# Fused attention and two MLPs on one core: k and q rows laid out consecutively per partition, transposes head by head, group sums of v by additions

## The chip, the cores and the metric

One core of a Trainium2 chip runs one launch. The metric is the device time of one execution in microseconds (us). All arrays are float32, except the weights and alpha, which are float64 and are read as pairs of 32-bit integers.

## What is computed

```python
q_d, k_d, v_d = q, k, v averaged over groups of 4 rows          # (4, 8, 144, 64)
out_up    = repeat(softmax(q_d k_d^T / 8) v_d, 4, rows)          # coarse attention
out_local = softmax(where(|i - j| < 4, q k^T / 8, -1e6)) v       # banded attention
x  = (out_up + out_local), heads side by side                    # (2304, 512)
x  = (silu(x w_gate) * (x w_val)) w_out                          # d_ff 1536
h  = x w_in                                                      # d_ff 2048
out = (max(h, 0) + alpha * min(h, 0)) w_out2                     # (2304, 512)
```

with q, k and v of shape (4, 8, 576, 64): four sequences, eight heads, 576 rows, 64 columns.

## The kernel before

**Units.** The attention is cut into 32 units. A unit n is one head pair (hp = n mod 4) of one block of 288 tokens; two blocks make a sequence. Units 0 to 3 are the first half of sequence 0, units 4 to 7 its second half. Units 0 to 7 run in a prologue, the others are woven into the first MLP's loop. A unit goes through these steps: `a_load` (k for the whole sequence if it is a first half, and q), `a_load_v` (v in groups of four rows), `a_load_w` (v in overlapping windows, L249, out of a DRAM copy `vwin`), `a_T` (k and q transposed, so that the 64 columns of two heads lie on 128 partitions; group sums kd and qd), `a_vd` (group sums of v), `a_QK` (L360 banded scores, L364 coarse scores), `a_EXP` (L394, L403), `a_NRM` (L427), `a_PT` (L441 transposes, L444 copies the coarse probabilities to SBUF on ACT), `a_PV` (L461 coarse, L465 banded product, then the sum L470 on DVE and the splitting into the high part xh, L474 on ACT, and the low part xl).

**Window copies.** `stage(b)` copies v of a sequence from DRAM to DRAM into overlapping windows (L260 and L266), 8 KB for each window. Those of sequence 0 come in the prologue, that of sequence 1 behind the load of block 7's w_out, those of sequences 2 and 3 behind the load of block 11's.

**Weights.** The first MLP has 12 weight blocks j, each with three tiles of 512 KB: g_j, v_j (L106) and o_j (L104). `w_split` prepares one: two activations on ACT (L129, L137), one operation on DVE, a cast on ACT (L142) and a subtraction on GpSimd, which leave the weight as the sum of two float32 replacements that TensorE takes at its fast rate. `m_g` multiplies by g_j (three matmuls of `mm3`, L488 to L490, for each of four pieces of 128 columns), takes tanh (L527) and a product u (L528, DVE); `m_v` and `m_y` follow with v_j and o_j. For the first 288 tokens, the blocks are used in order as they are prepared; for later tokens all are there.

**Slots.** The tiles of the prologue's attention lie in the SBUF slots of weight blocks 4 to 11, so those weights are loaded when the unit that held the slot is done with it (`pslot`). o11's slot belongs to no unit.

**The order of instructions.** The kernel is written in the order of the steps, but a list scheduler of the framework sets the order of each engine's queue, from its own estimate of durations; a few `issue_after` calls bind pieces of it (`gate`, `prep1`, `load8`). Each engine and each DMA-issuing queue then works through its list in order. All loads here are issued by SP (SyncE). A change of one step can therefore move instructions of all others.

**What the change touches.** The k loads (L213) and q loads (L218): one DMA for each head, in which partition p gets rows p, 96 + p, ... of the sequence, 64 numbers (256 bytes) in a piece. The transposes L306, L309 and L315 (one for both heads of 96 rows), and the copies out of PSUM behind them: L310 to L312 on ACT, L319 on DVE. The group sums of v, L344: two reductions on DVE for each of units 0 to 3.

Of the kernel before, what the change touches and what calls it, by code (L numbers as in the profile page):

```python
# [23 lines left out]
def attn_moe_moe2_kernel(  # L24
# [169 lines left out]
    def a_load(n):  # L194
        b, half, hp, blk = coords(n)
        h0, t0 = 2 * hp, half * HB
        d = hu[n] = {}
        if n >= NPRO:

            loads = [("qn", q, HB, t0)]  # L200
            if half == 0:
                loads.insert(0, ("kn", k, S, 0))
            for tag, src, rn, r0 in loads:
                t = d[tag] = ap_.tile([128, rn], F32, tag=tag, name=tag, bufs=1)
                for i in range(4):
                    nc.sync.dma_start(
                        out=t[32 * i:32 * (i + 1)].rearrange("r (m c) -> r m c", c=32),
                        in_=src[b, h0 + i // 2, r0:r0 + rn, 32 * (i % 2):32 * (i % 2 + 1)].rearrange("(m r) c -> r m c", r=32))
            return
        if half == 0:  # L210
            kn = d["kn"] = at_(n, [QB, 6, 2, D], "kn")
            for h in range(2):
                nc.sync.dma_start(out=kn[:, :, h], in_=k[b, h0 + h].rearrange("(r p) c -> p r c", p=QB))  # L213
        t = at_(n, [128, 2 * NW * 2 * D], "qv").rearrange("p (a w h c) -> p a w h c", a=2, w=NW, h=2)
        d["vw"] = t[:, 1]
        qn = d["qn"] = t[:QB, 0]
        for h in range(2):
            nc.sync.dma_start(out=qn[:, :, h], in_=q[b, h0 + h, t0:t0 + HB, :].rearrange("(r p) c -> p r c", p=QB))  # L218

    def a_load_v(n):  # L220
        b, half, hp, blk = coords(n)
# [30 lines left out]
    def stage(b, halves=(0, 1)):  # L252
# [32 lines left out]
        else:  # L285
            win(g0, g1)

    def a_T(n, A):
        b, half, hp, blk = coords(n)
        d = hu[n]  # L290
        idn = ident[:QB, :QB]
        small(n)
        qT, qd = d["qT"], d["qd"]
        nc.gpsimd.memset(qT[:, HB:HB + 8], 0.0)  # L294
        if half == 0:
            kT = kTs[hp] = ap_.tile([128, KW], F32, tag=f"kT{hp}", name="kT", bufs=1)
# [6 lines left out]
            nc.vector.transpose(out=qT[:, 0:HB], in_=d["qn"])  # L303
        elif half == 0:
            for r in range(6):
                nc.tensor.transpose(A[:, r // 3, (r % 3) * QB:(r % 3 + 1) * QB], d["kn"][:, r].rearrange("p h c -> p (h c)"), idn)  # L306
            for r in range(NW):
                dst = A[:, 1, HB + QB * r:HB + QB * (r + 1)] if r < 2 else A[:, 0, 320:320 + QB]
                nc.tensor.transpose(dst, d["qn"][:, r].rearrange("p h c -> p (h c)"), idn)  # L309
            nc.scalar.copy(out=qT[:, 0:2 * QB], in_=A[:, 1, HB:HB + 2 * QB])  # L310
            nc.scalar.copy(out=qT[:, 2 * QB:HB], in_=A[:, 0, 320:320 + QB])
            nc.scalar.copy(out=kT[:, 3:S + 3].rearrange("c (f t) -> c f t", f=2), in_=A[:, :, 0:HB])  # L312
        else:
            for r in range(NW):
                nc.tensor.transpose(A[:, 0, QB * r:QB * (r + 1)], d["qn"][:, r].rearrange("p h c -> p (h c)"), idn)  # L315
            if K["qtA"]:
                nc.scalar.copy(out=qT[:, 0:HB], in_=A[:, 0, 0:HB])
            else:
                nc.vector.tensor_copy(qT[:, 0:HB], A[:, 0, 0:HB])  # L319
        if half == 0:  # L320
            if 0 < n < NP:
                kq = kT[:, 3:S + 3].rearrange("c (g r) -> c g r", r=4)
# [13 lines left out]
    def a_vd(n):  # L336
# [2 lines left out]
            return  # L339
        if half == 0:  # L340
            vs = vss[hp] = ap_.tile([72, 2, 2, D], F32, tag=f"vs{hp}", name="vs", bufs=1)
            for f in range(2):
                if n < NP:
                    nc.vector.reduce_sum(vs[:, f], hu[n]["vd"][f].rearrange("p h (r c) -> p h c r", r=4), axis=AX.X)  # L344
                    continue
                vv = hu[n]["vd"][f].rearrange("p h (r c) -> p h r c", r=4)
                nc.gpsimd.tensor_tensor(out=vv[:, :, 0:2], in0=vv[:, :, 0:2], in1=vv[:, :, 2:4], op=ALU.add)
                nc.gpsimd.tensor_tensor(out=vs[:, f], in0=vv[:, :, 0], in1=vv[:, :, 1], op=ALU.add)
# [523 lines left out]
```

## Time and profile before

| | us |
|---|---|
| median of 3 runs | 1009.46 |
| lowest, highest | 1009.44, 1010.22 |
| the profiled execution's span | 1008.6 |
| PE (TensorE matmul) busy in it | 970.5 (96%) |
| DVE busy | 479.7 (48%) |
| ACT busy | 307.6 (30%) |
| POOL busy | 380.0 (38%) |

The profile gives the profiled execution's span and no other time of that execution. Of the span, some 160 us are the prologue and the first pass through the weight blocks, in which the attention of sequence 0, the loads and the preparation of the weights run side by side; behind it PE is nearly always busy. TensorE's granted clock is listed for each stretch as a share of its full rate.

### The profile page before, as it was taken

How to read it: one execution, taken by the hardware profiler on the slowest of the kernel's cores; microseconds unless marked ns; L12 is line 12 of the kernel's file. 1: busy time of each engine (PE TensorE's matmuls, PEld its weight loads, DVE VectorE, ACT ScalarE, POOL GpSimd, SP SyncE). 2: the span in 40 equal slices, each digit the busy share in tenths (PEclk: the TensorE clock that was granted, in tenths of full speed). 3: DMA queues.
4: the chain of work that ended last, by engine and by line, in shares of the span. 5: the costliest groups of instructions: out<-in, count | busy, mean ns of one | idle time of the engine just before them, and what ended most of it. 6: DMA issues, size and time to landing. Idle time of an engine off the chain costs nothing.

```text
span 1008.6 us, 19231 instructions
## 1 busy us (share of the span) xinstructions
PE 970.5 (96%) x7760; PEld 866.4 (86%) x7760; DVE 479.7 (48%) x1010; ACT 307.6 (30%) x699; POOL 380.0 (38%) x488
## 2 busy tenths in 40 slices
PE   5689899999999999999999999999999999999998
PEld 4488799999999999999999997888888888888897
DVE  5886874464535464545432769623222222322232
ACT  4598632222222222222223656312111111211111
POOL 6487852244322334222223436624223222322222
PEclk9799999999999999999999999999999999999999
DMA  7899731132111221111104883102000100100010
GB/s 185 254 337 340 174 89 35 27 82 56 41 38 33 70 45 41 44 23 21 41 9 141 287 255 106 32 1 79 6 0 21 53 1 1 47 7 0 1 43 21
DMA packets 135888, 77.80 MB, mean 77 GB/s; under 512 B 97401, under 2 KB 127097, under 8 KB 135033
## 3 DMA queue, kind: packets, MB, share of 16 engines
q1 hardware_dynamic: 135735, 76.57, 26.9%
q8 instruction: 60, 0.98, 0.4%
q14 instruction: 29, 0.24, 0.1%
q10 hardware_dynamic: 64, 0.01, 0.0%
HBM read 67.12 MB, written 15.73 MB: 82 GB/s over the span
## 4 chain that ended last, share of the span: by engine, by line
PE 81%; DMA 7%; DVE 4%; SPq 3%; POOL 2%; ACT 2%; issue 1%; POOLq 0%; DVEq 0%; ACTq 0%
PE y L625 7%; PE y L627 7%; PE y L626 7%; PE g L488 6%; PE v L489 6%; PE v L488 6%; PE g L489 6%; PE g L490 6%; PE v L490 5%; PE y L488 4%; PE y L490 4%; PE y L489 4%; PE h L488 3%; PE h L490 3%; PE h L489 3%; DMA raw<-in_moe_w_out_dram 3%
## 5 line engine op out<-in xcount | busy, mean ns | idle before, releaser
L613 POOL TENSOR_TENSOR gl<-t,gh 128x512 fp32r<-128x512 f32 (+1 forms) x80 | 97.1, 1214 | 250.6 <-ACT gh L612 244.3
L612 ACT CAST gh<-t 128x512 fp32r<-128x512 f32 (+1 forms) x80 | 46.1, 578 | 278.5 <-DVE t L609 238.8
L488 PE MATMUL g<-xh,w 128*128 128x288 f32 x384 | 117.7, 306 | 10.4 <-DVE u L528 5.4
L490 PE MATMUL g<-xh,w 128*128 128x288 f32 x384 | 115.0, 300 | 0.8 <-POOL qT L294 0.8
L488 PE MATMUL v<-xh,w 128*128 128x288 f32 x384 | 115.7, 301 | 0.1
L489 PE MATMUL v<-xl,w 128*128 128x288 f32 x384 | 115.1, 300 | 0.0
L489 PE MATMUL g<-xl,w 128*128 128x288 f32 x384 | 114.8, 299 | 0.0
L489 PE MATMUL y<-pl,w 128*128 128x288 f32 x384 | 113.9, 299 | 0.8 <-POOL pl L538 0.8
L625 PE MATMUL y<-w,gh 128*128 128x512 f32 x288 | 113.2, 393 | 1.0 <-ACT sy L557 1.0
L490 PE MATMUL v<-xh,w 128*128 128x288 f32 x384 | 113.3, 295 | 0.0
L490 PE MATMUL y<-ph,w 128*128 128x288 f32 x384 | 113.0, 297 | 0.0
L626 PE MATMUL y<-w,gh 128*128 128x512 f32 x288 | 112.8, 392 | 0.0
L627 PE MATMUL y<-w,gl 128*128 128x512 f32 x288 | 112.0, 392 | 0.0
L528 DVE SCALAR_TENSOR_TENSOR u<-u,g 128x288 f32<-128x288 f32 x96 | 43.3, 451 | 143.0 <-ACT u L527 142.9
L488 PE MATMUL y<-ph,w 128*128 128x288 f32 x384 | 110.9, 302 | 0.0
L538 POOL TENSOR_TENSOR pl<-u,ph 128x288 fp32r<-128x288 f32 x96 | 81.6, 850 | 56.9 <-ACT ph L537 56.5
L143 POOL TENSOR_TENSOR w<-st,w 128x512 fp32r<-128x512 f32 x52 | 70.7, 1366 | 55.6 <-ACT w L142 55.3
L488 PEld LDWEIGHTS g<-xh,w 128*128 128x128 f32 x384 | 73.3, 191 | 14.2 <-DVE u L528 7.4
L607 DVE TENSOR_SCALAR t<-h,alpha 128x512 f32<-128x512 f32 (+1 forms) x40 | 27.9, 696 | 110.7 <-PE h L490 109.5
L488 PEld LDWEIGHTS y<-ph,w 128*128 128x128 f32 x384 | 70.8, 189 | 4.5 <-issue 4.4
L490 PEld LDWEIGHTS g<-xh,w 128*128 128x128 f32 x384 | 73.6, 192 | 1.1 <-POOL qT L294 1.1
L527 ACT ACTIVATE u<-g 128x288 f32<-128x288 f32 x96 | 39.3, 409 | 115.4 <-PE g L490 109.3
(197 smaller groups left out, 2148.2 us busy)
## 6 DMA issues: line engine op xcount, KB each, us to landing
raw<-in_moe_w_out_dram SPq DMA_DIRECT2D x28, 512.0 KB
raw<-in_moe_w_in_dram SPq DMA_DIRECT2D x16, 512.0 KB
raw<-in_moe_w_gate_dram SPq DMA_DIRECT2D x12, 512.0 KB
raw<-in_moe_w_val_dram SPq DMA_DIRECT2D x12, 512.0 KB
vw<-vwin SPq DMA_DIRECT2D x48, 96.0 KB
out_dram<-os SPq DMA_DIRECT2D x18, 256.0 KB
sy<-y SPq DMA_DIRECT2D x16, 256.0 KB
y<-ys SPq DMA_DIRECT2D x14, 288.0 KB
```

The lines of the kernel that those rows point to most:

```text
L143: eng.tensor_sub(w[:, 1], st, f32(w[:, 0]))
L488: nc.tensor.matmul(o, lhi, rhi, start=first, stop=False)
L489: nc.tensor.matmul(o, lhi, rlo, start=False, stop=False)
L490: nc.tensor.matmul(o, llo, rhi, start=False, stop=last)
L527: nc.scalar.activation(out=u, in_=GV[0][:, :HB], func=AF.Tanh, scale=0.5)
L528: nc.vector.scalar_tensor_tensor(out=u, in0=u, scalar=1.0, in1=GV[0][:, :HB], op0=ALU.add, op1=ALU.mult)
L538: nc.gpsimd.tensor_sub(pl, u, f32(ph))
L612: nc.scalar.copy(out=gh[:, :n], in_=t[:, :n])
L613: nc.gpsimd.tensor_sub(gl[:, :n], t[:, :n], f32(gh[:, :n]))
L625: nc.tensor.matmul(o, gh[:, ms], ohi, start=(j == 0), stop=False)
L626: nc.tensor.matmul(o, gh[:, ms], olo, start=False, stop=False)
L627: nc.tensor.matmul(o, gl[:, ms], ohi, start=False, stop=(j == F2 - 1))
```

## The change

It alters three things. For units 0 to 7, k and q are loaded so that partition p holds consecutive rows (6p to 6p + 5 of k, 3p to 3p + 2 of q), one DMA for both heads of a unit, in pieces of 1536 and 768 bytes. Since the two heads of a row no longer lie side by side in a tile, each transpose of both heads becomes two ordinary matmuls against the identity, one for each head (`two_T`), and the copies out of PSUM write to strided places, which restores the order of the rows. For units 0 to 3, the two reductions of v become two additions of halves for the whole unit, in place and then into `vs`.

```diff
--- before.py
+++ after.py
@@ -208,14 +208,14 @@
                         in_=src[b, h0 + i // 2, r0:r0 + rn, 32 * (i % 2):32 * (i % 2 + 1)].rearrange("(m r) c -> r m c", r=32))
             return
         if half == 0:
-            kn = d["kn"] = at_(n, [QB, 6, 2, D], "kn")
-            for h in range(2):
-                nc.sync.dma_start(out=kn[:, :, h], in_=k[b, h0 + h].rearrange("(r p) c -> p r c", p=QB))
+            kn = d["kn"] = at_(n, [QB, 2, 6, D], "kn")
+            nc.sync.dma_start(out=kn.rearrange("p h r c -> p h (r c)"),
+                              in_=k[b, h0:h0 + 2].rearrange("h (p r) c -> p h (r c)", p=QB))
         t = at_(n, [128, 2 * NW * 2 * D], "qv").rearrange("p (a w h c) -> p a w h c", a=2, w=NW, h=2)
         d["vw"] = t[:, 1]
-        qn = d["qn"] = t[:QB, 0]
-        for h in range(2):
-            nc.sync.dma_start(out=qn[:, :, h], in_=q[b, h0 + h, t0:t0 + HB, :].rearrange("(r p) c -> p r c", p=QB))
+        qn = d["qn"] = t[:QB, 0].rearrange("p w h c -> p (w h c)").rearrange("p (h r c) -> p h r c", h=2, r=NW)
+        nc.sync.dma_start(out=qn.rearrange("p h r c -> p h (r c)"),
+                          in_=q[b, h0:h0 + 2, t0:t0 + HB, :].rearrange("h (p r) c -> p h (r c)", p=QB))
 
     def a_load_v(n):
         b, half, hp, blk = coords(n)
@@ -285,12 +285,17 @@
         else:
             win(g0, g1)
 
+    def two_T(dst, src, idn):
+        for h in range(2):
+            nc.tensor.matmul(dst[64 * h:64 * h + 64], src[:, h], idn, start=True, stop=True)
+
     def a_T(n, A):
         b, half, hp, blk = coords(n)
         d = hu[n]
         idn = ident[:QB, :QB]
         small(n)
         qT, qd = d["qT"], d["qd"]
+        qR = qT[:, 0:HB].rearrange("c (p r) -> c r p", r=NW)
         nc.gpsimd.memset(qT[:, HB:HB + 8], 0.0)
         if half == 0:
             kT = kTs[hp] = ap_.tile([128, KW], F32, tag=f"kT{hp}", name="kT", bufs=1)
@@ -303,20 +308,21 @@
             nc.vector.transpose(out=qT[:, 0:HB], in_=d["qn"])
         elif half == 0:
             for r in range(6):
-                nc.tensor.transpose(A[:, r // 3, (r % 3) * QB:(r % 3 + 1) * QB], d["kn"][:, r].rearrange("p h c -> p (h c)"), idn)
+                two_T(A[:, r // 3, (r % 3) * QB:(r % 3 + 1) * QB], d["kn"][:, :, r], idn)
             for r in range(NW):
                 dst = A[:, 1, HB + QB * r:HB + QB * (r + 1)] if r < 2 else A[:, 0, 320:320 + QB]
-                nc.tensor.transpose(dst, d["qn"][:, r].rearrange("p h c -> p (h c)"), idn)
-            nc.scalar.copy(out=qT[:, 0:2 * QB], in_=A[:, 1, HB:HB + 2 * QB])
-            nc.scalar.copy(out=qT[:, 2 * QB:HB], in_=A[:, 0, 320:320 + QB])
-            nc.scalar.copy(out=kT[:, 3:S + 3].rearrange("c (f t) -> c f t", f=2), in_=A[:, :, 0:HB])
+                two_T(dst, d["qn"][:, :, r], idn)
+            nc.scalar.copy(out=qR[:, 0:2], in_=A[:, 1, HB:HB + 2 * QB].rearrange("c (r p) -> c r p", r=2))
+            nc.scalar.copy(out=qR[:, 2], in_=A[:, 0, 320:320 + QB])
+            nc.scalar.copy(out=kT[:, 3:S + 3].rearrange("c (p f r) -> c f r p", f=2, r=NW),
+                           in_=A[:, :, 0:HB].rearrange("c f (r p) -> c f r p", r=NW))
         else:
             for r in range(NW):
-                nc.tensor.transpose(A[:, 0, QB * r:QB * (r + 1)], d["qn"][:, r].rearrange("p h c -> p (h c)"), idn)
+                two_T(A[:, 0, QB * r:QB * (r + 1)], d["qn"][:, :, r], idn)
             if K["qtA"]:
-                nc.scalar.copy(out=qT[:, 0:HB], in_=A[:, 0, 0:HB])
+                nc.scalar.copy(out=qR, in_=A[:, 0, 0:HB].rearrange("c (r p) -> c r p", r=NW))
             else:
-                nc.vector.tensor_copy(qT[:, 0:HB], A[:, 0, 0:HB])
+                nc.vector.tensor_copy(qR, A[:, 0, 0:HB].rearrange("c (r p) -> c r p", r=NW))
         if half == 0:
             if 0 < n < NP:
                 kq = kT[:, 3:S + 3].rearrange("c (g r) -> c g r", r=4)
@@ -339,10 +345,13 @@
             return
         if half == 0:
             vs = vss[hp] = ap_.tile([72, 2, 2, D], F32, tag=f"vs{hp}", name="vs", bufs=1)
+            if n < NP:
+                vv = vds[hp].rearrange("p h f (r c) -> p (h f) r c", r=4)
+                nc.vector.tensor_add(vv[:, :, 0:2], vv[:, :, 0:2], vv[:, :, 2:4])
+                vv = vds[hp].rearrange("p h f (r c) -> p f h r c", r=4)
+                nc.vector.tensor_add(vs, vv[:, :, :, 0], vv[:, :, :, 1])
+                return
             for f in range(2):
-                if n < NP:
-                    nc.vector.reduce_sum(vs[:, f], hu[n]["vd"][f].rearrange("p h (r c) -> p h c r", r=4), axis=AX.X)
-                    continue
                 vv = hu[n]["vd"][f].rearrange("p h (r c) -> p h r c", r=4)
                 nc.gpsimd.tensor_tensor(out=vv[:, :, 0:2], in0=vv[:, :, 0:2], in1=vv[:, :, 2:4], op=ALU.add)
                 nc.gpsimd.tensor_tensor(out=vs[:, f], in0=vv[:, :, 0], in1=vv[:, :, 1], op=ALU.add)
```

In the changed file the lines behind the first function move by a few numbers: L104 and L106 stay, L487 to L490 become L496 to L499, L444 becomes L453, L427 L436, L527 L536, L747 L756.

The change also moves instructions, since the scheduler orders them anew. On SP's queue, the rows behind the loads of weight blocks 0 and 1 (`raw` is a weight tile; `qv` of `vwin` are the window loads of units 4 to 7). Before, with raw_172, 174 and 176 for g2, v2 and o2, 178 to 182 for block 3, 913 and 915 for g4 and v4, and 1516 for o11:

```order
L249 DMA qv_149<-vwin_64 128x3x64 x2
L106 DMA raw_172<-in_moe_w_gate_dram 128x4x256
L106 DMA raw_174<-in_moe_w_val_dram 128x4x256
L104 DMA raw_176<-in_moe_w_out_dram 128x1024
L106 DMA raw_178<-in_moe_w_gate_dram 128x4x256
L106 DMA raw_180<-in_moe_w_val_dram 128x4x256
L104 DMA raw_182<-in_moe_w_out_dram 128x1024
L106 DMA raw_913<-in_moe_w_gate_dram 128x4x256
L106 DMA raw_915<-in_moe_w_val_dram 128x4x256
L747 DMA alpha_73<-in_moe2_alpha_dram 128x16x1
L104 DMA raw_1516<-in_moe_w_out_dram 128x1024
L260 DMA vwin_64<-in_v_dram 192x2048
```

and with the change, where raw_1552 is o11, 160 to 164 are g2, v2 and o2, and 166 to 170 block 3:

```order
L249 DMA qv_136<-vwin_64 128x3x64 x2
L756 DMA alpha_73<-in_moe2_alpha_dram 128x16x1
L104 DMA raw_1552<-in_moe_w_out_dram 128x1024
L260 DMA vwin_64<-in_v_dram 192x2048
L217 DMA qv_138<-in_q_dram 96x2x192
L249 DMA qv_138<-vwin_64 128x3x64 x2
L106 DMA raw_160<-in_moe_w_gate_dram 128x4x256
L106 DMA raw_162<-in_moe_w_val_dram 128x4x256
L104 DMA raw_164<-in_moe_w_out_dram 128x1024
L106 DMA raw_166<-in_moe_w_gate_dram 128x4x256
L106 DMA raw_168<-in_moe_w_val_dram 128x4x256
L104 DMA raw_170<-in_moe_w_out_dram 128x1024
```

Alpha, o11, the window copy of sequence 2 (192 pieces) and unit 7's q and window loads stood behind v4 and now stand ahead of g2. Behind the last row shown, the changed file has the copies of sequence 3 (L260 with 176 and 15 pieces, L283, L284), and then g4.

On ACT, the rows around unit 4's copy of probabilities (COPY qs<-att, L444 before and L453 in the changed file) and block 0's tanh (L527, L536). Before, with st_1000, 1007 and 1014 for g2, v2 and o2, and st_1065 for g3:

```order
L129 ACTIVATE st_1007<-raw 128x512
L137 ACTIVATE st_1007<-raw 128x512
L427 ACTIVATE qs<-qs,sr_81 72x144 x2
L142 CAST w<-st_1000 128x512
L129 ACTIVATE st_1014<-raw 128x512
L137 ACTIVATE st_1014<-raw 128x512
L527 ACTIVATE u<-g 128x288
L427 ACTIVATE qs<-qs,sr_82 72x144 x2
L444 COPY qs<-att 72x288
L142 CAST w<-st_1007 128x512
L129 ACTIVATE st_1065<-raw 128x512
L137 ACTIVATE st_1065<-raw 128x512
```

and with the change, with st_1101, 1108 and 1115 for g3, v3 and o3, and st_1166 for g4:

```order
L142 CAST w<-st_1101 128x512
L436 ACTIVATE qs<-qs,sr_81 72x144 x2
L129 ACTIVATE st_1115<-raw 128x512
L137 ACTIVATE st_1115<-raw 128x512
L536 ACTIVATE u<-g 128x288
L142 CAST w<-st_1108 128x512
L436 ACTIVATE qs<-qs,sr_82 72x144 x2
L129 ACTIVATE st_1166<-raw 128x512
L137 ACTIVATE st_1166<-raw 128x512
L453 COPY qs<-att 72x288
L142 CAST w<-st_1115 128x512
L453 COPY qs<-y_69 72x288
```

Before, unit 4's copy stood behind the preparation of o2; now it stands behind that of g4. In the changed file, g2's first activation stands right behind the cast of xh for unit 3, ahead of unit 4's exponentials.

## Rows read from the trace of the kernel before

**Rows 1.** Windows of the span: length, busy us (instructions) of each engine, granted clock, DMA share, GB/s

```profile
58.94:78.06 19.12, 19.02 (x200) 17.67 (x200) 15.23 (x33) 17.37 (x47) 17.08 (x19) 0.92 0.94 328
78.06:112.19 34.13, 29.90 (x264) 27.25 (x264) 23.28 (x36) 28.35 (x57) 27.83 (x24) 1.00 0.91 283
112.19:160.00 47.81, 44.69 (x423) 41.54 (x424) 36.44 (x78) 17.96 (x42) 29.95 (x39) 0.96 0.45 109
160.00:540.00 380.00, 380.00 (x4032) 361.91 (x4031) 184.17 (x485) 96.78 (x256) 118.48 (x202) 1.00 0.19 42
```

**Rows 2.** Timeline of PE, first gate matmul of blocks 0, 1, 2: start, length, idle before

```profile
47.66 0.61 PE L488 MATMUL g<-xh,w 128*128 128x288 f32 x1 [3.03 <-DVE qs L470]
...
58.94 0.61 PE L488 MATMUL g<-xh,w 128*128 128x288 f32 x1 [0.91 <-DVE u L528]
...
65.19 0.38 PE L488 MATMUL g<-xh,w 128*128 128x288 f32 x1
```

**Rows 3.** Timeline of ACT, 36 to 57 us: start, length, idle before and releaser

```profile
36.39 0.68 ACT L129 ACTIVATE st<-raw 128x512 f32<-128x512 f32 x1 [2.17 <-DMA raw<-in_moe_w_gate_dram]
...
46.75 0.69 ACT L129 ACTIVATE st<-raw 128x512 f32<-128x512 f32 x1
47.31 0.68 ACT L137 ACTIVATE st<-raw 128x512 int32<-128x512 uint8 x1
47.87 0.63 ACT L142 CAST w<-st 128x512 fp32r<-128x512 f32 x1
48.38 0.38 ACT L403 ACTIVATE qs<-qs 128x192 f32<-128x192 f32 x1
...
49.70 0.69 ACT L129 ACTIVATE st<-raw 128x512 f32<-128x512 f32 x1 [0.61 <-DMA raw<-in_moe_w_gate_dram]
...
56.60 0.40 ACT L444 COPY qs<-att 72x288 f32<-72x288 f32 x1
```

**Rows 4.** Timeline of SP's queue, from the first load to the first weight: start, length

```profile
0.74 0.94 SPq L213 DMA_DIRECT2D kn<-in_k_dram  x2
...
9.14 0.96 SPq L260 DMA_DIRECT2D vwin<-in_v_dram  x1
...
29.59 2.97 SPq L218 DMA_DIRECT2D qv<-in_q_dram  x6
32.60 0.47 SPq L106 DMA_DIRECT2D raw<-in_moe_w_gate_dram  x1
```

**Rows 5.** Windows, columns as in Rows 1, during the k and q loads and the first weights

```profile
4.00:8.00 4.00, 3.05 (x30) 2.43 (x38) 1.21 (x2) 1.00 (x3) 3.88 (x21) 1.00 1.01 215
36.00:40.00 4.00, 1.79 (x76) 1.18 (x76) 2.48 (x6) 2.91 (x5) 0.14 (x2) 0.79 1.06 373
```

**Rows 6.** Timeline of SP's queue, alpha's issue and the next

```profile
51.05 3.10 SPq L747 DMA_DIRECT2D alpha<-in_moe_alpha_dram  x1
54.20 6.41 SPq L104 DMA_DIRECT2D raw<-in_moe_w_out_dram  x1
```

**Rows 7.** Windows, columns as in Rows 1, around alpha's transfer and the one behind it

```profile
56.00:60.00 4.00, 2.62 (x28) 2.14 (x29) 3.69 (x10) 4.00 (x13) 3.66 (x4) 0.85 1.03 248
60.00:64.00 4.00, 4.00 (x28) 3.83 (x28) 3.86 (x9) 4.00 (x12) 3.34 (x4) 0.73 0.65 218
64.00:68.00 4.00, 4.00 (x91) 3.48 (x89) 3.71 (x9) 4.00 (x11) 3.78 (x4) 1.00 1.00 387
```

**Rows 8.** Timeline of PE, transposes of a unit and its banded product

```profile
11.23 1.17 PE L306 MATMUL gv<-ident,kn 96*128 96x96 f32 x6
...
41.73 1.17 PE L465 MATMUL gv<-bd,qv 128*64 128x96 f32 x12
```

**Rows 9.** Window, columns as in Rows 1, of the first 25 us

```profile
0.00:25.00 25.00, 14.73 (x256) 10.65 (x256) 13.10 (x45) 12.37 (x42) 16.91 (x52) 1.00 0.72 185
```

**Rows 10.** Timeline of DVE, the group sums of v of units 0 to 3

```profile
24.30 7.76 DVE L344 TENSOR_REDUCE vs<-vd 72x128 f32<-72x512 f32 x8
```

**Rows 11.** First line of the page

```profile
span 1008.6 us, 19231 instructions
```

## The prediction

> **What bounds the kernel now.** I read the windows first. From 160 to 540 us PE is busy for 380.00 of 380.00 us [rows 1], so nothing that happens before 160 us can be made up later: whatever PE loses or gains at the front is lost or gained at the end. Before that, PE idles 0.10 us in 58.94 to 78.06, 4.23 us in the next stretch (34.13 less 29.90) and 3.12 us in the one behind it (47.81 less 44.69): 7.35 us in all, the only place where a late front can be caught up.
>
> So the question is when PE's gate matmuls of weight blocks 0, 1 and 2 begin. They begin at 47.66, 58.94 and 65.19 us [rows 2]. Between 47.66 and 58.94 the engine to look at is ACT, which works in order. It gets block 2's first weight (g2) at 49.70 us after 0.61 us of waiting for that transfer, and copies unit 4's probabilities (L444) at 56.60 [rows 3]; PE's PV matmuls of unit 4 and then block 1's gate matmuls come 2.34 us later, 0.91 of it spent on the product u of block 0 [rows 2].
>
> **What the change does to the loads.** SP issues the k and q loads of units 0 to 3 in 16 instructions, from 0.74 us at 0.47 us each, and the first window copy at 9.14 [rows 4]. Eight remain, so that issue can move up by some 4 us. The data, 1.77 MB, moves at 215 GB/s (window 4 to 8 us), while whole weights move at 373 [rows 5]: 8.2 us now, 4.7 at the weights' rate. The new pieces (768 and 1536 bytes instead of 256) have no row. Bounds: nothing saved, and 3.5 us. I take 2.8 (330 GB/s), nearer the weights, whose pieces are the next in size. The Trainium skill ("DMA: Bandwidth & Descriptors", Specifications) puts line rate at pieces of 512 bytes and up; by that the saving is 3.5 and the sum below 0.7 lower.
>
> The first weight is issued at 32.60 us, behind six q loads of units 4 to 7 that take SP 2.97 us [rows 4]. Two remain there: 2.0 us less. Together with the issues saved ahead this puts the first weight at 32.60 − 2.0 − 2.8 to 4.4, that is 26.2 to 27.8; I take 26.2, as two q issues that stood among the window loads also go. So the weight stream starts 6.4 us earlier, and g0, which ACT got at 36.39 [rows 3], lands at 30.0.
>
> **What it does to the order behind.** A weight is 0.524 MB, 1.40 us at 373 GB/s. The six weights of blocks 0 and 1 are in by 37.4. But SP's order [the first pair of excerpts above] now has alpha, o11, the 192 window copies of sequence 2, unit 7's q and window loads **ahead of** g2; before, the six weights of blocks 2 and 3, g4 and v4 came first. Their prices:
> - six window loads at 215 GB/s, as small pieces: 2.7 us
> - alpha: SP's issue takes 3.10 us, and the next instruction on SP another 6.41 [rows 6]; meanwhile windows 56 to 60 and 60 to 64 carry 248 and 218 GB/s against 387 in the one behind them [rows 7]. Against 374 that is (126 + 156) x 4 us = 1.13 MB not moved: 3.0 us. Lower bound 0.5 (one issue), upper 6.4
> - o11: 1.4; the 192 copies, 1.57 MB at 387 GB/s: 4.1; unit 7's loads: 1.3
>
> So g2 lands at 37.4 + 2.7 + 3.0 + 1.4 + 4.1 + 1.3 + 1.4 = 51.3 (48.8 to 54.7 by alpha's bounds), later than today's 49.70 in spite of the head start. Then five weights (7.0) to o3 at 58.3, sequence 3's copies (4.1), g4 at 63.8.
>
> **What waits for that.** ACT's order [second pair] puts the preparation of g2, v2, o2, g3, v3, o3 **and g4** ahead of unit 4's copy (L453 in the new file); before only g2, v2 and o2 stood between. One preparation is two activations at a pitch of 0.56 us, and its cast L142 0.51 (47.87 to 48.38) [rows 3]. From g2's landing to the copy it was 6.90 us (49.70 to 56.60). Now add four pairs, 4.48, three casts, 1.53, and three exponentials that have moved in, 1.0: 13.9. The copy comes at 51.3 + 13.9 = 65.2 (g4's landing alone allows no less than 63.8 + 1.1). Block 0's tanh is long past, so of the 2.34 us from there to block 1 the 0.91 goes: block 1 starts at 65.2 + 1.4 = 66.6 us, against 58.94: **+7.7 us**. Behind the waiting ACT instruction stand unit 4's exponentials and all that follows, so PE has nothing to put there.
>
> Block 2's gate matmuls wait for block 1's tanh, which now stands behind g5's preparation. g5 is the seventh transfer of its run, 63.8 + 6 x 1.4 = 72.2; its pair 1.1, some 2.1 of other ACT work (two casts, a copy, a cast of xh, one activation, at the rows' pitches), tanh and product 0.8: 76.2 against 65.19, **+11.0 us**. From there PE is the bound: the granted clock was 0.92 (a mix of its two levels) in 58.94 to 78.06 and 1.00 (2.4 GHz) in the stretch behind it [rows 1], so I give back 1.0 (at most 0.08 x 19.12 = 1.5). Of the 7.35 us of idle time I take half as caught up, 3.7, because the weights of blocks 5 and up now land ahead of need; the bounds are none and all.
>
> **The edits in the units themselves.** One PE transpose becomes two matmuls. Six transposes take 1.17 us, and six fp32 matmuls of 96 columns (L465, twelve passes) also 1.17 us, 0.195 each [rows 8]. So each transpose costs 0.195 more: 36 of them for units 0 to 3, 7.0 us. PE is busy for 14.73 of its first 25 us [rows 9], so it is hidden, and it would cost at most 7.0 if nothing else were late; the cover is ACT, whose work ahead of g2 ends at 49.1 now (0.61 before 49.70), so some 6.4 earlier, and which then waits until 51.3. Twelve more stand in units 4 to 7; of those only unit 7's three lie where PE is the bound: +0.3 (0 to 0.6). The Trainium skill ("Perfetto Trace Analysis", Optimizing Tensor Performance) speaks against this edit: transposes instead of standard matmuls, and "TensorE: Matmul & The Clock Gate" (Terms) has them four times faster for fp32. The row of ordinary matmuls does not show that; it is rival 4.
>
> DVE's eight v-sums take 7.76 us from 24.30 on [rows 10]. Four additions over 512 and four over 256 elements have no row of this shape: between nothing and all of 7.76 saved; I take a quarter, 1.9, since they go over 768 places per unit where the reductions go over 1024. The strided copies on ACT go the other way, likewise at most some us. Either would start block 0 sooner or later, and both are hidden behind the same ACT wait for g2; without that wait they would be worth up to 4.
>
> **Sum.** 11.0 − 1.0 − 3.7 + 0.3 = +6.6 us on the profiled execution's span of 1008.6 [rows 11]: 1015.2. The median of the runs, 1009.46, is 0.9 above that span: **1016.0 us**. With none of the idle time caught up 1019.7, with all 1012.3; with alpha's bounds the case reaches 1011.6 to 1021.
>
> **Rivals.**
> 1. *The head start carries through* (faster). If g2 is there before 43.6 us, ACT's 13.9 us of work ends by 57.5 and block 1 starts no later than 58.94. For it: the stream starts 6.4 us earlier, and the last of block 1's weights is in at 37.4. Against it: 6.2 us would have to hold what costs 13.9 above; alpha and the window copies would have to run beside g2 and not ahead of it. Then the gain lies between the loads' 2.8 and the stream's 6.4: 5 us, 1004.5. 17 in 100.
> 2. *The slip is absorbed.* If block 1's tanh is not held by g5, the slip stays at +7.7, and the idle 7.35 us takes it up: 1009.46 + 0.4 = 1009.8. For it: three weights take 4.2 us to come, and a block's interval is 6.25 now (58.94 to 65.19), so a full queue gains on PE. Against it: g5's place in SP's order. 14 in 100.
> 3. *The loads do not get faster* though their pieces do grow: the 2.8 us are not saved, and everything stands that much later, 1018.8. For it: the loads fill 96 partitions, not 128, and SP's issue was nearly as long as the data. Against: the share of the DMA engines is 1.01 at 215 GB/s [rows 5], so pieces, not issue, fill them. 9 in 100.
> 4. *The matmuls are four times as slow as transposes*: 0.78 for each half, 1.37 more per transpose, 49 us for 36, less the 10.3 us of PE idle in the first 25 us: 39 us on units 0 to 3, around 1048. Against it stand the two like durations of [rows 8]; it is the Trainium skill's rule cited above. 2 in 100.
>
> **How the numbers follow.** The forecast case has 58 in 100, so the time is its sum, 1016.0. Within 0.2% (about what a measurement of this kernel can tell from no change) is 1007.4 to 1011.5: rival 2, 0.14. Faster is rival 1, 0.17; slower the rest, 0.69. The range is 1003.5 to 1020.5: below it lies half of the little-known end of rival 1, above it rival 4, part of rival 3 and the forecast's last microsecond, together under 2 in 10.
>
> **What would show it.** Right: SP's first weight issue at 25 to 28 us; alpha issued before 40; ACT's activation of g2 idle for a DMA of raw for several us, beginning near 43 and ending at 49 to 54; block 1's gate matmuls near 66, released by ACT; PE busy all of 160 to 540 as before. Wrong: g2's activation before 44 us (then rival 1), block 1 near 66 but block 2 within 7 us of it (rival 2), the first window copies not earlier than now (rival 3), or PE as the releaser of ACT in the first 30 us with the new matmuls at over 0.4 us each (rival 4).

## The result, and the profile after

| | before | changed |
|---|---|---|
| median, us (4 runs each) | 1009.45 | 1021.63 |
| lowest to highest | 1009.38 to 1010.22 | 1019.81 to 1023.89 |
| ratio, 95% interval | | 1.0116 (1.0101 to 1.0132) |
| profiled span | 1008.6 | 1021.8 |

The change costs 12.2 us where 6.6 were forecast, above the end of the range. The profiled execution was the slowest of the four (1023.89), so its span is 13.2 longer than the span of the profile before. First the windows of the changed kernel, with the columns of [rows 1]: length, busy us and instructions of PE, PEld, DVE, ACT and POOL, granted clock, DMA share, GB/s.

```profile
58.94:78.06 19.12, 11.95 (x140) 9.37 (x140) 16.07 (x42) 18.44 (x50) 16.18 (x20) 0.62 1.06 371
78.06:112.19 34.13, 29.51 (x278) 28.39 (x278) 22.49 (x41) 27.80 (x62) 27.60 (x25) 0.93 0.59 177
112.19:160.00 47.81, 44.67 (x410) 41.52 (x411) 37.22 (x70) 20.36 (x43) 32.77 (x40) 0.91 0.55 132
160.00:540.00 380.00, 380.00 (x4066) 361.74 (x4065) 188.90 (x500) 95.79 (x254) 115.96 (x202) 1.00 0.18 40
```

Behind 160 us nothing changes. The damage lies in 58.94 to 78.06, where PE idles 7.17 us against 0.10 in [rows 1], at a granted clock of 0.62 against 0.92, while ACT is busy for 18.44 of 19.12 us. On PE's timeline (start, length, idle before and releaser) these are its two longest waits there (6.25 of the 7.71 us lie ahead of 58.94), the first gate matmuls of blocks 0, 1 and 2 (L497), and the longest wait behind them:

```profile
46.84 0.40 PE L497 MATMUL g<-xh,w 128*128 128x288 f32 x1
...
60.40 0.46 PE L369 MATMUL y<-kT,qs 64*32 64x32 f32 x30 [7.71 <-DVE qs L325]
...
64.43 0.45 PE L450 MATMUL att<-ident,qs 72*72 72x72 f32 x2 [3.57 <-ACT qs L436]
...
70.39 0.61 PE L497 MATMUL g<-xh,w 128*128 128x288 f32 x1
...
81.69 0.44 PE L497 MATMUL g<-xh,w 128*128 128x288 f32 x1
...
112.57 0.69 PE L369 MATMUL att<-kT,qT 64*32 64x32 f32 x40 [3.91 <-DVE qT L308]
```

Against [rows 2], block 0 starts 0.8 us earlier, block 1 11.5 later, block 2 16.5 later. The 7.71 us end with a copy on DVE, qT of unit 6 (L325). On DVE's timeline it stands behind the operation on g2 (L139), which waits for ACT:

```profile
55.32 0.69 DVE L139 SCALAR_TENSOR_TENSOR st<-st 128x512 int32<-128x512 int32 x1 [8.68 <-ACT st L137]
...
59.81 0.53 DVE L325 COPY qs<-y 128x288 f32<-128x288 f32 x1
```

In the kernel before, that copy (L319 there) was done early:

```profile
48.42 0.44 DVE L319 COPY qs<-y 128x288 f32<-128x288 f32 x1
```

So DVE's new order, too, puts a unit behind the weights. ACT's timeline shows what stands between (L129 at 54.01 is g2, at 74.97 g5; L536 is tanh of blocks 0 and 1; L453 at 68.31 unit 4's copy):

```profile
46.68 0.43 ACT L483 CAST xh<-qs 128x288 fp32r<-128x288 f32 x1
54.01 0.66 ACT L129 ACTIVATE st<-raw 128x512 f32<-128x512 f32 x1 [6.90 <-DMA raw<-in_moe_w_gate_dram]
...
65.69 0.41 ACT L536 ACTIVATE u<-g 128x288 f32<-128x288 f32 x1
...
68.31 0.39 ACT L453 COPY qs<-att 72x288 f32<-72x288 f32 x1
...
74.97 0.68 ACT L129 ACTIVATE st<-raw 128x512 f32<-128x512 f32 x1
...
78.25 0.39 ACT L536 ACTIVATE u<-g 128x288 f32<-128x288 f32 x1
```

ACT waits 6.90 us for g2 (0.61 in [rows 3]), reaches the copy 14.3 us behind it (6.90 before), and tanh of block 1 after the preparation of g5. In the kernel before, that tanh (L527) came ahead of g4:

```profile
63.98 0.40 ACT L527 ACTIVATE u<-g 128x288 f32<-128x288 f32 x1
```

And SP's queue (start, length), with the first weight, alpha, o11, sequence 2's copies, g2, and unit 8's k loads:

```profile
26.63 0.45 SPq L106 DMA_DIRECT2D raw<-in_moe_w_gate_dram  x1
...
40.05 0.50 SPq L756 DMA_DIRECT2D alpha<-in_moe_alpha_dram  x1
40.59 1.41 SPq L104 DMA_DIRECT2D raw<-in_moe_w_out_dram  x1
42.04 0.57 SPq L260 DMA_DIRECT2D vwin<-in_v_dram  x1
...
45.11 1.21 SPq L106 DMA_DIRECT2D raw<-in_moe_w_gate_dram  x1
...
98.30 7.19 SPq L206 DMA_DIRECT2D kn<-in_k_dram  x4
```

Two things moved at once, then: g2's place on SP and the order on ACT (with DVE's). Either, or the edits in the units, might be the loss. The theories that the expectations number are: (1) the late g2 and ACT's order together, as forecast; (2) the late weights alone; (3) the units' own edits; (4) the ACT work put ahead of units 4 to 7, whose unit 7 then holds up unit 8's loads; (5) the scheduler's whole new order; (6) the order on the computing engines, with the loads second.

### The profile page after: what moved, and what is told of

It reads as the page before. It is cut to its first block, busy times and chain, and to the rows that moved or that the text cites. A ratio compares the mean times of both kernels' runs of the same rounds, so it can differ in the third digit from the quotient of the medians.

```text
span 1021.8 us, 19498 instructions
## 1 busy us (share of the span) xinstructions
PE 974.5 (95%) x7904; PEld 872.8 (85%) x7904; DVE 476.3 (47%) x1010; ACT 311.0 (30%) x699; POOL 381.4 (37%) x488
## 3 DMA queue, kind: packets, MB, share of 16 engines
q8 instruction: 62, 1.02, 0.4%
## 4 chain that ended last, share of the span: by engine, by line
PE 82%; DMA 7%; SPq 4%; DVE 2%; POOL 2%; issue 2%; ACT 1%; POOLq 0%; DVEq 0%; ACTq 0%
PE y L634 6%; PE y L636 6%; PE y L635 6%; PE g L497 6%; PE v L498 6%; PE v L497 6%; PE g L498 6%; PE g L499 6%; PE v L499 6%; PE y L497 5%; PE y L499 4%; PE y L498 4%; PE h L497 3%; PE h L499 3%; PE h L498 3%; DMA raw<-in_moe_w_val_dram 2%
## 5 line engine op out<-in xcount | busy, mean ns | idle before, releaser
L497 PE MATMUL g<-xh,w 128*128 128x288 f32 x384 | 117.3, 305 | 3.6 <-DVE u L537 3.3
L497 PE MATMUL v<-xh,w 128*128 128x288 f32 x384 | 115.1, 300 | 0.0
L499 PE MATMUL g<-xh,w 128*128 128x288 f32 x384 | 114.6, 298 | 0.0
L499 PE MATMUL y<-ph,w 128*128 128x288 f32 x384 | 113.8, 299 | 0.0
L499 PE MATMUL v<-xh,w 128*128 128x288 f32 x384 | 113.2, 295 | 0.0
L537 DVE SCALAR_TENSOR_TENSOR u<-u,g 128x288 f32<-128x288 f32 x96 | 43.4, 452 | 147.8 <-ACT u L536 147.8
L497 PE MATMUL y<-ph,w 128*128 128x288 f32 x384 | 111.5, 303 | 0.0
L547 POOL TENSOR_TENSOR pl<-u,ph 128x288 fp32r<-128x288 f32 x96 | 79.4, 827 | 56.2 <-ACT ph L546 55.8
L497 PEld LDWEIGHTS g<-xh,w 128*128 128x128 f32 x384 | 73.7, 192 | 6.3 <-DVE u L537 4.9
L536 ACT ACTIVATE u<-g 128x288 f32<-128x288 f32 x96 | 39.3, 409 | 120.8 <-PE g L499 120.7
L498 PEld LDWEIGHTS g<-xl,w 128*128 128x128 f32 x384 | 73.6, 192 | 2.6 <-POOL xl L484 2.4
L497 PEld LDWEIGHTS y<-ph,w 128*128 128x128 f32 x384 | 71.0, 189 | 4.7 <-issue 4.4
```

The source lines that it names most:

```text
L497: nc.tensor.matmul(o, lhi, rhi, start=first, stop=False)
L498: nc.tensor.matmul(o, lhi, rlo, start=False, stop=False)
L499: nc.tensor.matmul(o, llo, rhi, start=False, stop=last)
L536: nc.scalar.activation(out=u, in_=GV[0][:, :HB], func=AF.Tanh, scale=0.5)
L537: nc.vector.scalar_tensor_tensor(out=u, in0=u, scalar=1.0, in1=GV[0][:, :HB], op0=ALU.add, op1=ALU.mult)
L547: nc.gpsimd.tensor_sub(pl, u, f32(ph))
```

## The experiments

**One place put back at a time.** These kernels bind pieces of the changed kernel's order. *hold* puts alpha, o11 and the copies behind v4 again; ACT's order stays that of the changed kernel.

```diff
-        nc.sync.dma_start(out=alpha_sb, in_=alpha.rearrange("(j p) -> p j", p=128))
+        with tc.issue_after(wdma["v4"]):
+            nc.sync.dma_start(out=alpha_sb, in_=alpha.rearrange("(j p) -> p j", p=128))
...
-                        load1(F1 - 1)
+                        with tc.issue_after(wdma["v4"]):
+                            load1(F1 - 1)
```

> The changed kernel, with the issue of alpha and of the last block's weights bound behind v4's load, so that SP again loads g2, v2, o2, block 3, g4 and v4 ahead of alpha, o11 and the window copies; ACT's order stays row for row that of the changed kernel. Theory 1 (g2 late, and ACT's order puts all of blocks 2, 3 and g4 ahead of unit 4's copy: both are needed for the loss): g2 reaches ACT near 46 us instead of 54.01, unit 4's copy comes 14 us behind it, block 1 starts near 62 instead of 70.39, and the end is 1007 to 1013. Theory 2 (late weights alone starve PE, whatever ACT's order): within 2 us of before, 1007 to 1011. Theory 3 (the doubled matmuls, strided copies and lower clock of the units themselves cost): 1018 to 1022, as the changed kernel.

*act* puts ACT's preparation of block 2 behind unit 4's copy and that of block 3 behind unit 5's; *both* is hold and act together.

```diff
+            if j in {2: 4, 3: 5}:
+                es.enter_context(tc.issue_after(gates["A", {2: 4, 3: 5}[j], 2]))
...
+            gate(n, 2)
```

> The changed kernel, with ACT's preparation of block 2 bound behind unit 4's copy of probabilities and that of block 3 behind unit 5's; SP's order stays that of the changed kernel, so g2 still lands near 54 us. Theory 1: units 4 and 5 are done without waiting for g2, block 1 starts near 56 us, block 2 near 60, and the end is 1004 to 1011. Theory 2: PE is short of weights from block 2 on all the same, 1016 to 1021. Theory 3: 1018 to 1022.

> Both bindings together: the weights ahead of alpha, o11 and the copies, and ACT's units ahead of blocks 2 and 3. Theory 1: the head start of the loads carries through, g2 at ACT near 46 us, block 1 near 56, and the end is 1002 to 1008, below before. Theory 2: as with the first binding alone, 1007 to 1011. Theory 3: 1018 to 1022.

Measured, as ratios to the kernel before: hold 1.0127 (1.0110 to 1.0144), act 1.0123 (1.0107 to 1.0139), both 1.0139 (1.0124 to 1.0153). None gives anything back. In microseconds they are 1022.34, 1022.88 and 1024.17: theory 1 misses all three, theory 2 too, and by the times alone theory 3 would be near. ACT in hold, at the preparation of g2, unit 4's copy, and g5:

```profile
49.39 0.68 ACT L129 ACTIVATE st<-raw 128x512 f32<-128x512 f32 x1 [0.77 <-POOL w L143]
...
64.70 0.37 ACT L453 COPY qs<-att 72x288 f32<-72x288 f32 x1
...
75.16 0.66 ACT L129 ACTIVATE st<-raw 128x512 f32<-128x512 f32 x1 [3.75 <-DMA raw<-in_moe_w_gate_dram]
```

The 6.90 us of waiting for g2 are gone, and the copy comes only 3.6 earlier, since ACT still has the same work ahead of it. Then the wait stands at g5, which tanh of block 1 stands behind: block 2 starts at 81.14, hardly before the changed kernel's 81.69. Theory 2 falls, and with it the step on which the forecast's block 1 rested, and so does theory 1 as it was put. In both, block 2 does start at 69.05, but then ACT has gaps:

```profile
53.01 0.36 ACT L412 ACTIVATE qs<-qs 128x192 f32<-128x192 f32 x1 [2.84 <-POOL qs L395]
...
55.48 0.38 ACT L403 ACTIVATE qs<-y,nb 72x144 f32<-72x144 f32 x1 [2.11 <-DVE sr L425]
...
58.85 0.72 ACT L436 ACTIVATE qs<-qs,sr 72x144 f32<-72x144 f32 x2 [1.39 <-DVE sr L425]
59.48 0.37 ACT L453 COPY qs<-att 72x288 f32<-72x288 f32 x1
59.76 0.66 ACT L129 ACTIVATE st<-raw 128x512 f32<-128x512 f32 x1
```

Block 2's preparation begins at 59.76, 10.1 us behind [rows 3], and the blocks fall behind one by one: block 8 starts at 117.68 and block 12, the first block of the next 288 tokens, at 149.68 (103.75 and 134.00 in the kernel before). In the changed kernel ACT did preparation in the gaps of the units' chains; with the bound, the gaps stay empty.

*holdact* is hold with block 3's preparation alone behind unit 4's copy (`{3: 4}` in place of `{2: 4, 3: 5}`).

> The changed kernel with SP's order held as in the run hold, and on ACT only block 3's preparation bound behind unit 4's copy, so that g2, v2 and o2 stand ahead of it and g3 behind it, as in the kernel before. Theory 4: ACT does not stand idle as in the run both, unit 4's copy comes at 57 to 60, unit 7's cast at 88 to 92, and the end is 1006 to 1012. Theory 3: 1018 to 1023.

1.0083 (1.0069 to 1.0096), 1018.21 us: the best of the four, though theory 4 had 1006 to 1012 and theory 3's range holds it. Blocks 1 and 2 start at 60.06 and 66.19, 1 us behind the kernel before, and 7.2 us are lost behind them.

**The two moves put into the kernel before.** *early* writes alpha, o11 and sequence 2's copies ahead of block 2's weights; *prepfirst* puts ACT's preparation of blocks 2 and 3 ahead of unit 4's copy and leaves SP alone. Both edits are shown in part.

```diff
...
+                if tok == "2":
+                    with tc.issue_after(wdma["o1"]):
+                        nc.sync.dma_start(out=alpha_sb, in_=alpha.rearrange("(j p) -> p j", p=128))
+                        w_load("o", F1 - 1, f"o{F1 - 1}")
+                        stage(2)
...
```
```diff
-... pre=(0, 2, 0, 0) ...
+... pre=(0, 4, 0, 0) ...
+                if n == NP:
+                    es.enter_context(tc.issue_after(acts[-2]))
             a_PT(n, A)
```

> The kernel before, with alpha, o11 and sequence 2's window copy issued ahead of g2, as in the changed kernel, and nothing else changed by hand; the scheduler, which sees the late loads, puts unit 4's and 5's copies ahead of block 2's preparation. So it has late weights and the old units. Theory 1: g2 lands near 59 us, but block 1 starts by 60, so the loss is under half of the changed kernel's: 1009 to 1014. Theory 2: 1018 to 1025, since its weights are later still than those of the changed kernel. Theory 3: 1008 to 1011.

> The kernel before, old loads, old transposes and old sums, with SP's order as it was; the preparation of blocks 2 and 3 is written ahead of units 4 to 7, and unit 4's copy of probabilities is bound behind the second activation of o3, which is where the changed kernel has it but for one more weight. Theory 4 (ACT's order, which puts preparation ahead of units 4 to 7, is the loss by itself, wherever the loads stand; unit 7's xh cast, 89.1 us before and 99 in both changed kernels with that order, then holds unit 8's loads): unit 4's copy near 68, unit 7's cast at 96 to 101, the end 1015 to 1022. Theory 3 (the units' own edits): 1008 to 1012.

early 1.0055 (1.0041 to 1.0069), prepfirst 1.0057 (1.0041 to 1.0074): under half of the loss each, with blocks 1 and 2 at 59.94 and 66.01, and at 58.70 and 65.88, nearly in time. At 1015.74, early lies outside the ranges of theories 1, 2 and 3; prepfirst, at 1014.70, just misses theory 4's and is outside theory 3's. A small disturbance of the order anywhere seemed to cost some 5 us.

**The edits one by one.** *vsum* is the kernel before with the additions of v alone; *kq* is the changed kernel with the old reductions.

```diff
-                if n < NP:
-                    nc.vector.reduce_sum(vs[:, f], hu[n]["vd"][f].rearrange("p h (r c) -> p h c r", r=4), axis=AX.X)
-                    continue
+            if n < NP:
+                ...
+                nc.vector.tensor_add(vv[:, :, 0:2], vv[:, :, 0:2], vv[:, :, 2:4])
+                ...
+                nc.vector.tensor_add(vs, vv[:, :, :, 0], vv[:, :, :, 1])
+                return
```

> The kernel before with the sums of v as additions of halves, and nothing else. DVE has a few us less to do, but the scheduler's order now has unit 4's copy behind all six preparations of blocks 2 and 3 instead of three, and o11 and the window copies ahead of v4. Theory 4: slower all the same, 1013 to 1020. Theory 3 (no matmul or strided copy was touched): 1006 to 1010.

> The changed kernel with the old reductions of v: the loads, the two matmuls and the strided copies are in. SP's order has alpha, o11 and the copies ahead of g2 as in the changed kernel, but on ACT unit 4's copy stands behind four preparations and not seven. Theory 4: unit 4's copy near 62 to 65, the end 1010 to 1016, less than the changed kernel's. Theory 3: 1018 to 1023, as the changed kernel.

vsum 1.0046 (1.0034 to 1.0058), kq 1.0115 (1.0098 to 1.0132). vsum, at 1014.79, is as theory 4 said and not as theory 3; kq, at 1021.48, is the reverse. Eight additions in the place of eight longer reductions make the kernel slower: that is hardly their own price, and the scheduler had given each of these kernels another order. So the order itself had to be held.

**Edits and order taken apart.** A table of instruction numbers per engine and a chain of issue-order bounds (they add no wait between engines) fix the queues of all five engines for the first 160 us or so. *pin* is the changed kernel, with all its edits, in the order of the kernel before (the two half matmuls where the transpose stood, an addition where a reduction stood, a merged load where the first of its two stood). *unpin* is the kernel before in the changed kernel's order. *vsum_pin* and *kq_pin* are the edits one by one in the order of the kernel before.

```diff
+    traced = {i.name: i for i in tc.nc.cur_bb.bb.instructions}
+    for name, text in PIN.items():
+        ...
+        chain = [traced[f"I-{n}"] for n in ids if f"I-{n}" in traced]
+        for a, z in zip(chain, chain[1:]):
+            tc.add_manual_dep(z, a.name, info, reason="pin")
```

> The changed kernel, all three edits in, with the instructions of the first 160 us of all five engines queued in the order of the kernel before (a table of their places; behind it the scheduler's own choice came out the same). A pair of matmuls stands where a transpose stood, a merged load where the first of its two stood. Theory 5 (the scheduler's new order is the whole loss, on all engines together, so that no single binding undoes it): 1004 to 1010, as before or a little faster. Theory 3 (the edits themselves: doubled matmuls, strided copies, larger descriptors): 1017 to 1022, as the changed kernel.

> The kernel before, none of the edits in, with its instructions queued in the order of the changed kernel on all five engines. Theory 5: 1018 to 1024, the changed kernel's loss without its edits, or more, as the old loads are slower. Theory 3: 1008 to 1012.

> The sums of v as additions alone, in the order of the kernel before. Theory 5: the 4.6 us that the run vsum lost are gone, 1006 to 1010. Theory 3 has nothing for this edit to lose but the additions themselves: if they are slower than the reductions, 1011 to 1015.

> The loads of k and q, the matmuls and the strided copies, with the old sums of v, in the order of the kernel before. Theory 5: 1005 to 1011, within 2 us of the run pin. Theory 3: 1017 to 1022.

| ratio (interval) | order before | the changed order |
|---|---|---|
| no edits | 1 | unpin 1.0162 (1.0149 to 1.0175) |
| v additions | vsum_pin 0.9998 (0.9989 to 1.0006) | |
| k, q loads and matmuls | kq_pin 0.9999 (0.9991 to 1.0008) | |
| all edits | pin 0.9968 (0.9956 to 0.9980) | the change 1.0116 (1.0101 to 1.0132) |

This settles the question between edits and order. The new order costs 15.7 us without any edit (1025.52 against 1009.82), the edits in the old order gain 2.8 (1007.04), and with the edits in, the new order costs 14.6 (1021.63 against 1007.04). Theory 5 holds in all four (unpin is 1.5 above its 1018 to 1024, which it gave with "or more"; kq_pin, 1009.62, is 2.6 from pin and not within 2); theory 3 falls. The same lines in unpin, ACT at g2 and at unit 4's copy, then PE at block 1:

```profile
56.62 0.66 ACT L176 ACTIVATE st<-raw 128x512 f32<-128x512 f32 x1 [8.09 <-DMA raw<-in_moe_w_gate_dram]
...
71.17 0.39 ACT L491 COPY qs<-att 72x288 f32<-72x288 f32 x1
...
73.25 0.61 PE L535 MATMUL g<-xh,w 128*128 128x288 f32 x1
```

In pin, ACT at g2, unit 4's copy, tanh of block 1 and g5 (with no wait), and PE at blocks 0 to 2:

```profile
47.26 0.69 ACT L178 ACTIVATE st<-raw 128x512 f32<-128x512 f32 x1
...
54.18 0.38 ACT L502 COPY qs<-att 72x288 f32<-72x288 f32 x1
...
61.53 0.40 ACT L585 ACTIVATE u<-g 128x288 f32<-128x288 f32 x1
...
75.48 0.70 ACT L178 ACTIVATE st<-raw 128x512 f32<-128x512 f32 x1
```
```profile
45.16 0.61 PE L546 MATMUL g<-xh,w 128*128 128x288 f32 x1 [2.84 <-DVE qs L528]
...
56.52 0.61 PE L546 MATMUL g<-xh,w 128*128 128x288 f32 x1 [0.95 <-DVE u L586]
...
63.09 0.38 PE L546 MATMUL g<-xh,w 128*128 128x288 f32 x1
```

All but g5 stand 2.1 to 2.5 us ahead of the kernel before ([rows 2 and 3], and 63.98 for the tanh), and tanh of block 1 comes 14.0 us ahead of g5 rather than 3.3 behind it. The gain needs both edits: in vsum_pin the sums are short but ACT waits for the first weight until 36.71, as in [rows 3]; in kq_pin the weights are early but the sums end only at 35.73 (27.94 + 7.79, against 32.06 in [rows 10]) and block 0 starts at 48.69.

```profile
36.71 0.66 ACT L178 ACTIVATE st<-raw 128x512 f32<-128x512 f32 x1 [3.77 <-DMA raw<-in_moe_w_gate_dram]
```
```profile
27.94 7.79 DVE L399 TENSOR_REDUCE vs<-vd 72x128 f32<-72x512 f32 x8
```

**SP's order and the computing engines' order apart**, with all edits. *lateloads* has SP in the changed order and PE, ACT, DVE and POOL in that of the kernel before; *earlyloads* is the reverse. Only the table of numbers differs from pin.

> The changed kernel with the four computing engines (PE, ACT, DVE, POOL) queued in the order of the kernel before, and SP in the order of the changed kernel: alpha, o11 and the window copies ahead of g2. Theory 6 (the order of the computing engines carries the loss): g2 lands near 54 us, unit 4's copy comes 6.9 us behind it near 61, block 1 near 63, but the weave behind it holds: 1010 to 1015. Theory 1 (the late weights carry it): 1016 to 1022.

> The changed kernel with SP queued in the order of the kernel before, g2 to v4 ahead of alpha, o11 and the copies, and the four computing engines in the order of the changed kernel. Theory 6: 1017 to 1022, no better than the changed kernel, as in the run hold. Theory 1: 1007 to 1011.

| with all edits, ratio (interval) | SP as before | SP as changed |
|---|---|---|
| computing engines as before | pin 0.9968 | lateloads 1.0042 (1.0028 to 1.0056) |
| computing engines as changed | earlyloads 1.0104 (1.0087 to 1.0121) | the change 1.0116 |

In microseconds: 1007.04, 1013.86, 1020.39 and 1021.63. The computing engines' order alone costs 13.4, SP's alone 6.8, and SP's on top of the other 1.2, which is not told apart from nothing (the intervals 1.0087 to 1.0121 and 1.0101 to 1.0132 overlap). Theory 6 holds in both runs, theory 1 in neither. Why they don't add can be read on ACT. In lateloads the wait for g2 is nearly as long as in the changed kernel, but unit 4's copy (59.05) follows 6.85 us behind g2, and blocks 1 and 2 start only 2.3 and 2.5 us behind the kernel before:

```profile
52.20 0.66 ACT L178 ACTIVATE st<-raw 128x512 f32<-128x512 f32 x1 [6.63 <-DMA raw<-in_moe_w_gate_dram]
```
```profile
61.22 0.61 PE L546 MATMUL g<-xh,w 128*128 128x288 f32 x1
...
67.71 0.40 PE L546 MATMUL g<-xh,w 128*128 128x288 f32 x1 [0.36 <-DVE u L586]
```

In earlyloads g2 is in time, the copy still comes 15.3 us behind it, and at g5 ACT waits for the transfer, with tanh of block 1 (L584) behind; block 2 starts at 80.40:

```profile
47.64 0.67 ACT L177 ACTIVATE st<-raw 128x512 f32<-128x512 f32 x1 [0.74 <-POOL w L191]
...
62.97 0.37 ACT L501 COPY qs<-att 72x288 f32<-72x288 f32 x1
...
74.42 0.66 ACT L177 ACTIVATE st<-raw 128x512 f32<-128x512 f32 x1 [4.76 <-DMA raw<-in_moe_w_gate_dram]
...
77.67 0.40 ACT L584 ACTIVATE u<-g 128x288 f32<-128x288 f32 x1
```

ACT gets to g5 at 74.42 here, after a wait, and at 74.97 in the changed kernel, without one; in both, tanh of block 1 comes 3.3 behind. So with this order of the computing engines block 2 comes late whether g2 is in time (80.40) or not (81.69). That g5's place alone does it is read from the two traces; no run moved it alone.

## Why the prediction was right and wrong

**Right: the place and the direction.** The stretch was 58.94 to 78.06, PE is busy for all of 160 to 540, SP's first weight is issued at 26.63 (forecast 26.2, 25 to 28), alpha at 40.05 (before 40, but for 0.05), and ACT waits several us for g2 (from 47.1, not 43). From g2 to unit 4's copy it was 14.3 us for 13.9 forecast.

**Mis-sized: the slip at block 2, 11.0 forecast and 16.5 measured.** Term by term: g2 reached ACT at 54.01, not 51.3, within alpha's bounds (+2.7: alpha's term was about right, see below, and which of the other transfers ran over was not tried). The copy followed at 68.31 for 65.2 (+3.1 in all), and block 1 2.1 behind it rather than 1.4: 70.39 for 66.6 (+3.8). Two misses make up the 5.5 us of the slip. ACT got to g5 at 74.97 for 72.2, without a wait for the transfer, and so tanh of block 1 came at 78.25 for 75.4 (76.2 less 0.8 for tanh and product): +2.8. From that tanh to block 2 it was 3.4 us, not 0.8: +2.6. The product (L537) came on DVE only at 79.64, behind other work, and on PE the scores of unit 7 (released at 79.11 by DVE) and the y matmuls of block 0 (80.17 to 81.69) stand ahead. The sum had taken only ACT for that step.

**Mis-sized: what is caught up.** 1.0 for the clock and 3.7 of idle time were given back. The slip fell to 14.2 at block 6 (105.03 against 90.85), rose to 19.5 at block 7 and 20.6 at block 8 (124.30 against 103.75), then fell to 14.6 at block 12 and 13.2 at the end: 3.3 of 16.5 recovered. The clock, a gain in the sum, went the other way: in 58.94 to 78.06, with 7.17 us of idle PE, 0.62 was granted for 0.92 (a mix of 1.2 and 2.4 GHz in both). And between blocks 6 and 7 PE met one wait that the sum did not have, 3.91 us at 112.57 for unit 8's qT, whose k loads were issued at 98.30 to 105.5 (from 89.19 before). Whether that late issue alone made the rise is open: unit 7's cast of xh, 89.10 in the kernel before, came at 99.18 in the changed one; in act and both it was back at 92.63 and 91.50, and they lost as much, while prepfirst had 101.17 and lost 4.7. In hold the cast was late as well (99.05), without such a rise (the slip is 14.8 at block 7), and the end as late.

**The step that failed: "so g2 lands at ... later than today's 49.70", with the wait for g2 as first term of the sum.** In the changed kernel it is there, but it is not what the loss hangs on. With g2 in time, hold and earlyloads still lose 12.1 and 10.5 us; with the old order of the computing engines, a late g2 (lateloads) costs 6.8 us against pin and 4.0 against the kernel before. The second half of the step, ACT's preparation ahead of unit 4's copy and tanh behind g5, was read rightly, and with the rest of the computing engines' order it is enough without a late g2: in earlyloads block 2 slips by 15.2 of the 16.5 us. That order alone costs 13.4 us. Which of the moved instructions carries them is not settled: the order of PE, ACT, DVE and POOL was tested as a whole, and each binding on ACT moved their other instructions too. DVE's share, which the prediction did not look at, is open too: its wait at g2 is 8.68 us in the changed kernel and 2.54 in earlyloads, and the end is nearly the same.

**Wrong in size but hidden: the units' edits.** A pair of half matmuls costs 0.365 us in the first six, a transpose 0.198 (24 passes in 2.19 against six transposes in 1.19), +0.167 for 0.195 forecast; the next six pairs take 1.78. Rival 4's four-fold is excluded.

```profile
4.47 2.19 PE L290 MATMUL att<-ident,kn 96*64 96x96 f32 x24 [4.47 <-POOL bd L689]
...
7.37 1.78 PE L290 MATMUL y<-ident,kn 96*64 96x96 f32 x24
```

For unit 7, at a granted clock of 1.00, the three pairs take 0.67 in pin and the three transposes 0.47 in the kernel before, +0.2 for the sum's +0.3. "Perfetto Trace Analysis" (Optimizing Tensor Performance) in the Trainium skill wants transposes in place of standard matmuls; here each half took 0.7 to 0.9 of the whole transpose's time, so the measured ratio, 1.4 to 1.8, comes of splitting it in two.

The additions of v take 4.3 us in pin (27.90 to 32.21, with L399 and L401 four times each) for the 7.76 of [rows 10], so some 3.4 saved and not 1.9:

```profile
27.90 0.68 DVE L399 TENSOR_TENSOR vd<-vd 72x512 f32<-72x512 f32 x1
28.61 0.42 DVE L401 TENSOR_TENSOR vs<-vd 72x256 f32<-72x256 f32 x1
```

The sums and copies were to be "worth up to 4" without the wait for g2; all edits together are worth 2.8 in pin. **Rival 1** is pin: its mechanism, the head start carried through, works when the order stays, and was forecast at 5. **Rival 2** named the right question, whether block 1's tanh is held by g5: it is. **Rival 3** was largely true in its premise: the last piece of k and q moves, by the traces' packets, only 0.7 to 0.8 us earlier (10.1 in the changed kernel and 10.0 in pin for 10.8), not 2.8, and the data did not reach the 330 GB/s assumed; yet the first weight was issued as early as forecast, with fewer issues ahead of it.

**Two slips in the sum's own working.** Six weights at 1.40 us behind the first one's 30.0 are in by 37.0, not 37.4. And the bounds that it gives, 3.4 more for alpha and 3.7 with nothing caught up, reach 1023.1 and not 1021; the measured 1021.63 lies inside its terms, though above the stated range.

## What to carry to other kernels

Where a list scheduler sets the queues, an edit's own price and the order that it brings are two changes: measure the edit with the old order pinned before judging it, and the new order without the edit. Read the order of the engine that feeds the bottleneck, and ask of each instruction that releases it (here tanh of a block) behind how many preparations of later blocks it stands. None of the four kernels here with one or two pieces bound back undid the order: in hold the computing engines kept it, and in act, both and holdact, with a bound on ACT, the scheduler rearranged the queues of all four of them.

## What the hardware showed

**Larger pieces helped less than thought.** Over 4 to 8 us, the stretch of [rows 5], the changed kernel carries 210 GB/s and pin 246, against 215 with pieces of 256 bytes. The windows 6 to 8 us, with pieces of 768 and 1536 bytes, reach 268 and 265, against 373 with weights. "DMA: Bandwidth & Descriptors" (Specifications) in the Trainium skill puts line rate at pieces of 512 bytes and up; the trace shows about seven tenths of the weights' rate.

```profile
6.00:8.00 2.00, 2.00 (x29) 2.00 (x28) 0.00 (x0) 0.35 (x2) 1.88 (x13) 1.00 1.12 268
```

**Strided copies out of PSUM** cost ACT nearly double here: the copy of kT (128 x 576) takes 1.20 us where the plain one took 0.66.

**Alpha** took SP 0.50 us to issue and the next instruction 1.41, where [rows 6] had 3.10 and 6.41: the same issue had two prices at two moments. The data behind it flowed as slowly as before, though: the window 40 to 44 us, with alpha, o11 and the first copies, carries 118 GB/s, and the next 406.

```profile
40.00:44.00 4.00, 4.00 (x52) 3.84 (x49) 2.85 (x7) 4.00 (x10) 4.00 (x4) 0.50 0.77 118
44.00:48.00 4.00, 4.00 (x115) 3.13 (x115) 2.02 (x3) 3.09 (x7) 4.00 (x5) 0.73 1.05 406
```

Against 373 GB/s, (373 - 118) x 4 us is 1.02 MB not moved, or 2.7 us, beside the 3.0 that the sum had taken from [rows 7].
